# Keeping TensorE on one kind of work between score groups, with 38 late groups in place of 37

## The chip, the cores and the metric

The kernel runs on one core of a Trainium2 chip, in one launch. The metric is the device time of that launch in microseconds. The kernel before takes 457.41 us, the median of 4 runs (457.12 to 457.46).

## The reference

One layer norm feeds two branches, whose results are multiplied. x is 2048 x 448 in bf16, there are 16 heads of 28, and the hidden layer of the second branch has 1792 columns.

```python
xn = layernorm(x)
# branch A: attention
q, k, v = split(xn @ wqkv)                 # 16 heads of 28
p = softmax(q @ k.T * 28 ** -0.5)          # 16 x 2048 x 2048
s = concat_heads(p @ v) @ wo
# branch B: dense, gelu, dense, silu
h = gelu(xn @ w1 + b1)                     # 2048 x 1792
g = silu(h @ w2 + b2)
out = x + s * g
```

## The kernel before

**Tiling.** The queries stand in 4 chunks of 512 columns, the heads in 4 groups of 4 heads (a head takes 32 partitions). One group with one chunk is a block, so there are 16 blocks. A block has 64 score tiles of 128 keys x 512 queries (16 key tiles for each of 4 heads), 1024 in the whole kernel, numbered m. Four tiles in a row, one key tile for the four heads, make a group of four, and there are 256 such groups.

**The exp of a tile** is made in one of two ways. On ScalarE (ACT) one ACTIVATE (L1305, `p_exps`) reads two or three PSUM banks of `ring` and writes as many tiles of P in bf16 (the names P, h and xnT on that line are three places where P slots lie). The ring is split into a set of three banks and a set of two; `p_scores` fills them in turn, and this is called a unit here. The score matmuls (L1249, in `t_score`) of the two or three tiles use different rows of the array and run beside each other. The groups of four that are listed in `QUADS` go the other way, called late groups here: `p_late` brings their four scores into single banks, VectorE (DVE) turns each into a linear form (L1408), and four wide DVE operations of a group (L1468, L1470, L1471, L1472) make three arrays whose sum is the approximate exp; GpSimd (POOL) prepares scaled values of v for them (L1480).

**The other work on TensorE (PE).** `pv_task` and `t_pv` add P times v into the bank `acc` (L1544); a late group takes three products per tile there in place of one. At the end of a block DVE copies `acc` (L1597) and a small chain normalises it (L1604, L1607, L1619, L1626). The first dense layer is L1111, its gelu L1160 on ACT; the second dense layer is L1181, followed by a Tanh on ACT (L1197) for the silu; the q and k projections are L758, v is L1049. The output projection is L1636; DVE multiplies (L1645) and adds x (L1649), and a DMA stores (L1651, L1653). The last block is cut into parts of 256, 128 and 128 queries, whose ends are L1571, L1582, L1585, L1588. L919 is a filler of three matmuls that adds zeros to `acc`; the planner puts it where its own account of PE shows little recent work.

**What sets the order.** The program is planned when it is built. Each piece of work is a generator that offers one `_Task` at a time, with an engine, a duration, a priority (`prio`, smaller is more urgent) and for PE a mode: "row" for scores (four rows of 32), "col" for L1544 and some small sums (four columns of 32), "full" for the rest. `start_of` gives the time at which a task could start by the planner's own account; a change of mode on PE adds `SWITCH` = 0.1 us to it. `run` takes the earliest task, looks at all tasks of that engine that could start within `EPS` = 0.1 us of it, and puts the one with the smallest priority into the engine's program. `pe_mode` is the mode of the last task put on PE. Priorities on PE: unit scores 1, single late scores 0.9, L1544 is 1.2 when it presses (many tiles behind, the end of the kernel, or near the gelu) and 6 otherwise, the first projections 1.5 and 1.6, most of the dense work and L1636 5, L919 95. Every engine runs its own program in order, and semaphores carry the dependencies.

```python
            s0, p0 = min(cand, key=lambda c: (c[0], c[1][3].prio, c[1][0], c[1][1]))
            E = p0[3].E
            near = [c for c in cand if c[1][3].E == E and c[0] <= s0 + EPS]
            s, p = min(near, key=lambda c: (c[1][3].prio, c[1][0], c[0], c[1][1]))
```

Of the kernel before, what the change touches and what calls it, by code (L numbers as in the profile page):

```python
# [11 lines left out]
PE, ACT, DVE, POOL, SP = ET.PE, ET.Activation, ET.DVE, ET.Pool, ET.SP  # L12
# [15 lines left out]
MTOT = NBLK * T * 4  # L28

GM = 64 * 9 + 6  # L30
QUADS = (17, 22, 24, 33, 39, 49, 52, 66, 75, 87, 88, 100, 101, 114, 124, 133, 138, 142, 146, 153, 154, 157, 161, 162, 171, 178, 179, 189, 194, 201, 205, 210, 216, 225, 231, 238, 243)
SM_SCALE = DH ** -0.5
LOG2E = 1.4426950408889634
EXP_C, EXP_LC = 0.1669921875, 1.1155446
# [44 lines left out]
class _Kernel:  # L79
# [132 lines left out]
    def run(self):  # L212
        idle = 0
        while True:
            self.settle()
            if not self.procs:
                return
            cand = []
            for p in self.procs:
                if isinstance(p[3], _Task):  # L220
                    s = self.start_of(p[3])
                    if s is not None:
                        cand.append((s, p))
            if not cand and idle < 100:
                idle += 1
                self.now += 0.1
                continue
            if not cand:
                raise RuntimeError("stuck at %.1f: %s" % (self.now, [(p[0], p[3] if not isinstance(p[3], _Task) else "task") for p in self.procs][:20]))
            s0, p0 = min(cand, key=lambda c: (c[0], c[1][3].prio, c[1][0], c[1][1]))  # L230
            E = p0[3].E
            near = [c for c in cand if c[1][3].E == E and c[0] <= s0 + EPS]
            s, p = min(near, key=lambda c: (c[1][3].prio, c[1][0], c[0], c[1][1]))
            if E == PE and p[3].prio >= 90:
                soon = [c for c in cand if c[1][3].E == PE and c[1][3].prio < 90 and c[0] <= s + p[3].dur]
                if soon:
                    s, p = min(soon, key=lambda c: (c[0], c[1][3].prio))
            idle = 0
            self.now = max(self.now, s)
            self.put(p[3], s)  # L240
            self.advance(p)

    def pe_free(self):
        return self.pe_wait == 0 or not self.late_on

    def ready(self, toks, ahead=0.0):
        return all(b.tw is not None and b.tw <= self.now + ahead for b in toks)

    def build(self):
        nc = self.nc  # L250
        with self.es:
            for E, nm in ((PE, "ev_pe"), (ACT, "ev_act"), (DVE, "ev_dve"), (POOL, "ev_pool"), (SP, "ev_sp")):
                self.evsem[E] = self.sem(nm)
                self.evcnt[E] = 0
            self.alloc()
            self.schedule()
            block = self.es.enter_context(nc.Block())
            for E, attr in ((SP, "sync"), (POOL, "gpsimd"), (DVE, "vector"), (ACT, "scalar"), (PE, "tensor")):
                lst = self.prog[E]

                def run(eng, lst=lst):
                    for f in lst:
                        f(eng)
                getattr(block, attr)(run)
# [129 lines left out]
    def schedule(self):  # L394
# [28 lines left out]
        K.pv_done = [False] * MTOT  # L423
        K.late = {4 * q + k for q in QUADS for k in range(4)}
        K.late_left = [sum(1 for q in QUADS if K.sub_of(4 * q) == b) for b in range(NBLK + 3)]
        K.late_on = False
# [951 lines left out]
    def p_late(self):  # L1378
        K = self
        yield ("until", lambda: K.late_on)  # L1380
        K.spawn(K.p_room(), 0)
        for q in QUADS:
            m0 = 4 * q
# [49 lines left out]
    def assign(self, ms, b0):  # L1433
        K = self
        n = len(ms)
        runs = [list(range(i, i + n)) for i0, w in K.pon for i in range(i0, i0 + w - n + 1)]
        run = min(runs, key=lambda x: (max(K.plast.get(i, -1) for i in x), x[0]))
        for i, m in zip(run, ms):
            K.PB[m] = i
            K.PPREV[m] = K.plast.get(i)  # L1440
            K.plast[i] = m
        K.units.append((ms, b0, run[0]))
# [287 lines left out]
```

## Time and profile before

| | |
|---|---|
| median of 4 runs | 457.41 us |
| the profiled execution: its own time, its span | 457.12 us, 455.3 us |
| ACT busy | 441.2 us (97%), 403 instructions |
| PE busy | 429.1 us (94%), 4389 matmuls |
| DVE busy | 369.6 us (81%), 576 instructions |
| POOL busy | 69.6 us (15%) |
| exps on ACT (L1305) | 195 of two banks, 162 of three |
| filler matmuls on PE (L919) | 357, 30.7 us busy |
| mean granted TensorE clock | 0.996 |

The span is the time from the first instruction to the last in the profiled execution; 1.8 us of the launch lie around it. Busy times of one engine count time in which at least one of its instructions is under way. Instructions of ACT and PE overlap with the next one at their ends, so the mean duration of a row is longer than the distance from one to the next.

### The profile page before, as it was taken

The page shows a single profiled execution, that of the slowest core. Times are in us where ns is not written, and L with a number is a line of the kernel's source. Part 1 is how long each engine was busy: PE and PEld are TensorE (multiplying, and loading weights), DVE is VectorE, ACT ScalarE, POOL GpSimd, SP SyncE. Part 2 cuts the span into 40 slices and gives each one's busy share as a digit, 9 for nine tenths or more (in the row PEclk, how much of TensorE's full clock was granted, in tenths as well). Part 3 has the DMA queues.
Part 4 walks back from the last instruction along what each step waited for, and adds up shares of the span by engine and source line. Part 5 has one row for each costly group of instructions (what it writes and reads, how often), then busy time and mean ns, then how long its engine had stood idle before and what let it go on. Part 6 is the DMA issues. An engine that isn't in the chain of part 4 may idle for free.

```text
span 455.3 us, 10592 instructions
## 1 busy us (share of the span) xinstructions
PE 429.1 (94%) x4389; PEld 160.3 (35%) x4419; DVE 369.6 (81%) x576; ACT 441.2 (97%) x403; POOL 69.6 (15%) x121
## 2 busy tenths in 40 slices
PE   6999999999999999999999999999999999989994
PEld 5543323333233332322334343343332333333552
DVE  8956898958979697968789997078899889888866
ACT  6999999999999999999999999999999999999993
POOL 7470100110020100100000030020011100212210
PEclk9999999999999999999999999999999999999998
DMA  8701000000000000000031000000000000212031
GB/s 277 254 3 37 1 0 1 1 12 2 3 1 0 1 1 3 2 1 1 1 111 35 2 0 1 1 2 0 1 1 2 1 1 8 53 25 42 2 43 42
DMA packets 8049, 11.16 MB, mean 25 GB/s; under 512 B 1697, under 2 KB 6993, under 8 KB 7954
## 3 DMA queue, kind: packets, MB, share of 16 engines
q1 hardware_dynamic: 6850, 8.43, 5.9%
q0 software_dynamic: 864, 1.38, 2.3%
q8 instruction: 35, 0.57, 0.5%
q10 hardware_dynamic: 288, 0.69, 0.4%
q14 instruction: 12, 0.10, 0.1%
HBM read 8.61 MB, written 3.21 MB: 26 GB/s over the span
## 4 chain that ended last, share of the span: by engine, by line
PE 60%; ACT 26%; issue 9%; DVE 3%; DMA 1%; POOL 0%; ACTq 0%; DVEq 0%; POOLq 0%
PE ring L1249 17%; ACT P L1305 14%; PE acc L1544 12%; ACT h L1305 8%; PE ring L1111 7%; PE misc L1181 5%; PE ring L1181 3%; ACT xnT L1305 3%; PE acc L919 2%; PE misc L1111 2%; PE misc L758 2%; PE ring L758 2%; PE ring L1636 2%; PE misc L1636 1%; PE misc L1049 1%
## 5 line engine op out<-in xcount | busy, mean ns | idle before, releaser
L1305 ACT ACTIVATE P<-ring 128x1024 bf16<-128x1024 f32 (+1 forms) x187 | 216.7, 1273 | 1.4 <-PE ring L1249 0.8
L1249 PE MATMUL ring<-qT,kT 32*128 32x512 bf16 (+2 forms) x1084 | 144.9, 358 | 10.7 <-ACT P L1305 3.9
L1305 ACT ACTIVATE h<-ring 128x1024 bf16<-128x1024 f32 (+1 forms) x102 | 118.6, 1269 | 0.4 <-PE ring L1249 0.2
L1249 PEld LDWEIGHTS ring<-qT,kT 32*128 32x128 bf16 x1084 | 37.3, 91 | 133.9 <-ACT P L1305 55.7
L1305 ACT ACTIVATE xnT<-ring 128x1536 bf16<-128x1536 f32 (+1 forms) x68 | 78.7, 1286 | 0.0
L1544 PE MATMUL acc<-P,vaug 128*32 128x512 bf16 (+2 forms) x530 | 49.3, 355 | 0.2 <-DVE E_sb L1597 0.2
L1480 POOL TENSOR_SCALAR cv<-vaug 128x128 bf16<-128x128 bf16 x38 | 26.5, 698 | 134.3 <-PE acc L1544 132.5
L1609 POOL CAST rhi<-rc 128x16 bf16<-128x16 f32 x15 | 7.9, 529 | 202.5 <-DVE rc L1607 168.2
L1111 PE MATMUL ring<-xnT,w 128*128 128x512 bf16 x139 | 35.8, 380 | 2.1 <-issue 1.4
L919 PE MATMUL acc<-ident,zero 128*128 128x128 bf16 x357 | 30.7, 221 | 0.0
L1544 PE MATMUL acc<-h,vaug 128*32 128x512 bf16 x248 | 28.4, 385 | 0.3 <-DVE E_sb L1597 0.3
L1181 PE MATMUL misc<-w,h 128*128 128x448 bf16 x112 | 26.9, 355 | 0.0
L1181 PE MATMUL ring<-w,h 128*128 128x448 bf16 x112 | 26.9, 355 | 0.0
L1249 PE MATMUL misc<-qT,kT 32*128 32x512 bf16 (+1 forms) x68 | 25.3, 377 | 0.0
L919 PEld LDWEIGHTS acc<-ident,zero 128*128 128x128 bf16 x357 | 20.4, 98 | 13.7 <-issue 12.5
L1111 PE MATMUL misc<-xnT,w 128*128 128x512 bf16 x68 | 19.1, 382 | 0.3 <-issue 0.2
L1111 PEld LDWEIGHTS ring<-xnT,w 128*128 128x128 bf16 x152 | 12.2, 97 | 17.7 <-issue 5.6
L1544 PEld LDWEIGHTS acc<-P,vaug 128*32 128x32 bf16 x530 | 12.4, 95 | 15.1 <-issue 12.5
L1544 PE MATMUL acc<-xnT,vaug 128*32 128x512 bf16 (+2 forms) x222 | 17.5, 332 | 0.0
L1408 DVE TENSOR_SCALAR w<-ring 128x512 uint16<-128x512 f32 x17 | 11.7, 686 | 5.8 <-PE ring L1249 5.8
L1160 ACT ACTIVATE h<-h 128x2048 bf16<-128x2048 bf16 (+2 forms) x8 | 16.2, 2020 | 0.0
L1408 DVE TENSOR_SCALAR x_sb<-ring 128x512 uint16<-128x512 f32 x19 | 13.1, 688 | 3.8 <-PE ring L1249 3.6
(284 smaller groups left out, 683.1 us busy)
## 6 DMA issues: line engine op xcount, KB each, us to landing
w<-in_B_w_dram SPq DMA_DIRECT2D x1, 1568.0 KB, 7.2
w<-in_B_w_dram SPq DMA_DIRECT2D x1, 1344.0 KB, 8.2
out_dram<-in_A_x_dram SPq DMA_DIRECT2D x3, 448.0 KB, 10.7
out_dram<-h POOLq DMA_DIRECT2D x6, 224.0 KB, 3.7
x_sb<-in_A_x_dram SPq DMA_DIRECT2D x2, 448.0 KB, 4.6
h<-in_A_wqkv_dram SPq DMA_DIRECT2D x3, 168.0 KB, 4.8
x_sb<-in_A_x_dram ACTq DMA_DIRECT2D x1, 448.0 KB, 4.3
h<-in_A_x_dram SPq DMA_DIRECT2D x1, 448.0 KB, 3.4
```

The costliest lines, as they stand in the source:

```text
L758: ins = eng.matmul(bank, w[:, kt, g * 128:(g + 1) * 128], K.xnT[:, kt, c * 512:(c + 1) * 512], start=(kt == 0), stop=(kt == KT - 1))
L919: ins = eng.matmul(K.acc[:, 0:128], K.zero[:, :], K.ident[:, :], start=False, stop=True, skip_group_check=True)
L1111: ins = eng.matmul(bank, K.w1[:, kt, ft * 128:(ft + 1) * 128], K.xnT[:, kt, c * 512:(c + 1) * 512], start=(kt == 0), stop=(kt == KT - 1))
L1160: yield _Task(ACT, lambda eng, dst=dst, src=src: eng.activation(dst, src, ACTF.Gelu_apprx_tanh), rd, wr, 0.4267 * n + (0.1 if pc else 0.06 ...
L1181: ins = eng.matmul(ps, hv[:, ft, t * 128:(t + 1) * 128], K.w2[:, ft, :], start=(ft == 0), stop=(ft == FT - 1))
L1249: return eng.matmul(dst, K.kT[32 * j:32 * j + 32, g, t * 128:(t + 1) * 128], K.qT[32 * j:32 * j + 32, g, c * 512 + q0:c * 512 + q0 + nq], ...
L1305: return eng.activation(reg[:, i0:i0 + n, :], K.ring[:, b0:b0 + n, :], ACTF.Exp, scale=SM_SCALE)
L1408: yield _Task(DVE, lambda eng: eng.tensor_scalar(K.unit[u][:, 512 * k:512 * k + 512].bitcast(dt.uint16), bank, SM_SCALE * LOG2E * 128.0, ( ...
L1480: yield _Task(POOL, lambda eng, i=i, t=t: eng.tensor_scalar(K.cv[:, i, :], K.vaug[:, t, 4 * g:4 * g + 4, :].rearrange("p h e -> p (h e)"), ...
L1544: return eng.matmul(K.acc[32 * j:32 * j + 32, q0:q0 + nq], w, ap[:, col:col + nq], tile_position=(0, 32 * j), start=(t == 0), stop=(t == T ...
L1609: yield _Task(POOL, lambda eng: eng.tensor_copy(K.rhi[:, :], K.rc[:, :]), [K.b_rc], [K.b_rhl], 1.1, 0.0, 1)
L1636: ins = eng.matmul(ps, K.qT[:, g, c * 512 + t * 128:c * 512 + (t + 1) * 128], K.wo[:, g, :], start=(g == 0), stop=(g == G - 1))
```

## The change

In `run`, the choice among the tasks that could start at about the same time goes by `rate` in place of `prio`. For a PE task with a priority between 1 and 90 (unit scores, single late scores and fillers are not among them), when the last PE task was no score and had another mode than this one, 4 is added. So after L1544 a waiting task of mode "full" counts 4 worse, and after a task of mode "full" a waiting L1544 does, whether it presses or not. After a score all is as before. `QUADS` is a new list with 38 groups in place of 37.

```diff
-QUADS = (17, 22, 24, 33, 39, 49, 52, 66, 75, 87, 88, 100, 101, 114, 124, 133, 138, 142, 146, 153, 154, 157, 161, 162, 171, 178, 179, 189, 194, 201, 205, 210, 216, 225, 231, 238, 243)
+QUADS = (17, 20, 21, 34, 39, 50, 52, 66, 74, 89, 98, 100, 107, 117, 120, 134, 139, 143, 146, 152, 154, 155, 157, 159, 162, 173, 177, 178, 188, 193, 198, 209, 211, 216, 226, 230, 234, 243)
...
-            s, p = min(near, key=lambda c: (c[1][3].prio, c[1][0], c[0], c[1][1]))
+            s, p = min(near, key=lambda c: (self.rate(c[1][3]), c[1][0], c[0], c[1][1]))
...
+    def rate(self, t):
+        p = t.prio
+        if t.E == PE and 1 < p < 90 and self.pe_mode != "row" and t.mode != self.pe_mode:
+            p += 4
+        return p
```

The lines behind the new function stand 6 lines lower in the kernel after (L1249 becomes L1255, L1305 becomes L1311, L1636 becomes L1642).

## The prediction

> **What bounds the kernel now.** I read the page first, then the waits of ACT and of all engines, then the chain and the timeline of single stretches. The page's first lines:
>
> ```profile
> span 455.3 us, 10592 instructions
> PE 429.1 (94%) x4389; PEld 160.3 (35%) x4419; DVE 369.6 (81%) x576; ACT 441.2 (97%) x403; POOL 69.6 (15%) x121
> ```
>
> Both ACT and PE look full. The table of waits, for ACT alone and then for all engines, parts them:
>
> ```profile
> ACT P L1305 <- PE ring L1249: 0.8, 2, 0.5
> ACT P L1305 <- PE misc L1249: 0.2, 1, 0.2
> ACT h L1305 <- PE ring L1249: 0.2, 1, 0.2
> ...
> PEld ring L1249 <- ACT P L1305: 55.7, 137, 0.8
> PEld ring L1249 <- ACT h L1305: 35.3, 84, 0.7
> PEld ring L1249 <- ACT xnT L1305: 20.0, 50, 1.2
> ```
>
> Among the exps ACT waits for scores 1.2 us in all. PE waits 111 us before scores, until an exp has read the banks. So the end is set by a row of 357 exps on ACT; PE sets it only where a score comes late. The pitch of that row comes from the ACT timeline at the end of the kernel (start, length, count of a merged row):
>
> ```profile
> 437.87 8.23 ACT L1305 ACTIVATE P<-ring 128x1536 bf16<-128x1536 f32 x7
> 445.92 2.01 ACT L1305 ACTIVATE xnT<-ring 128x1024 bf16<-128x1024 f32 x2
> 447.73 0.66 ACT L1213 ACTIVATE w<-w 128x448 bf16<-128x448 bf16 x1
> ```
>
> Two exps of two banks take 2.01, and one alone 1.08 (mean of its rows): the second costs about 0.92. The seven before start 8.05 ahead of the next row; four have three banks and three two, so one of three banks costs (8.05 - 3 x 0.91) / 4 = 1.33. Over the whole trace, from end to end, the usual pitch is 0.916 and 1.343. What lies above that pitch, the late scores, is about 3.5 us in all (gelu stretch left out).
>
> How a late score comes about is seen in the chain between 109.7 and 111.8 us, beside ACT's timeline row:
>
> ```profile
> 109.25 4.94 ACT L1305 ACTIVATE h<-ring 128x1536 bf16<-128x1536 f32 x4
> ...
> 109.73 0.32 PE ring L1249 x2
> 110.05 0.97 PE ring L1111 x4
> 111.02 0.43 PE misc L1111 x2
> 111.45 0.32 PE ring L1249 x3
> ```
>
> Between two unit scores PE does six L1111, 1.40 us; with the score 1.72. The four exps (3, 2, 3, 2 banks) would take 1.33 + 0.91 + 1.33 + 1.08 = 4.65 and took 4.94. The same rows price a change of mode: four L1111 after a score take 0.97, two after their like 0.43, so 0.97 - 0.86 = 0.11 for the change.
>
> The tail, from the last exp on, is the end of the chain (there every link counts):
>
> ```profile
> 445.92 1.10 ACT xnT L1305
> ...
> 447.07 1.31 PE ring L1636 x6
> 448.38 0.59 PE acc L1544 x32
> 448.99 0.30 DVE E_sb L1571
> ...
> 449.61 0.97 DVE w L1585
> ...
> 452.23 0.55 DVE h L1645
> 452.77 0.02 issue
> 452.79 0.39 DVE h L1649
> ```
>
> The last exp ends at 447.94, the last DVE operation at 453.2: 5.26 us. The last store ends the span at 455.3.
>
> **The change part by part.** The counts after are read from the instruction order of the two built programs.
>
> *Exps.* 38 groups leave 872 tiles to ACT, not 876: 355 exps in place of 357, two of the two-bank form fewer. 2 x 0.916 = 1.83 us less. Nothing else on ACT changes but the places of the four Tanh (each 5 to 9 exps later). Term: -1.8.
>
> *DVE and POOL.* One group more is four L1408 at 0.69, two operations at 0.69 (L1468, L1472) and two at 1.22 (L1470, L1471), 6.6 us, and one L1480 at 0.70 on POOL. DVE goes to 376 of 454 us. Hidden by DVE's own 86 us of idle time; its buffer is that a late group's sum is taken into `acc` later in its block. If that cover were gone where the groups now stand denser (six between 152 and 162, the second dense layer's stretch), the price is one group, 6.6 us on DVE, some of it seen by PE; the planner's order shows no exp waiting for DVE. Taken as 0.
>
> *L1544.* Eight products more, 4 side by side at 0.216: 0.43 us of PE. Off the path except by late scores.
>
> *Changes of mode.* They fall from 788 to 773. 15 x 0.11 = 1.6 us of PE. The filler L919 stays at 357 matmuls. PE already waits 111 us for ACT, so this is time that becomes waiting: 0 on the path, with -1.6 as its bound if every one stood before a late score. The page "TensorEngine Tiling (Array Packing)" of the Trainium skill says, under Tiling Modes, that a change of tiling mode drains TensorE; this trace shows 0.11 us. Taken alone the rule would credit all 15 and give -1.6 more; the waits above say why I don't.
>
> *Late scores.* I add up, for each pair of successive unit scores, the PE work that is queued between them, by the rows' prices (L1111 and L758 0.216, L1181 and L1636 0.19, four L1544 0.216, L1049 task 0.65 or 0.45, L919 task 0.17, a change of mode 0.11, a score 0.21). Queued on PE behind such work is the unit's score, and ACT waits for that. Leaving out stretches beside a Tanh or the gelu, where ACT gives time, the heavy intervals (1.6 us or more) are:
> before: four of 1.71 to 1.72, which cost 0.07, 0.22, 0.06, 0.15 (mean 0.125); eight of 1.61 to 1.62, which cost 0.65 together (mean 0.08). Sum 1.15.
> after: one of 1.84, five of 1.71 to 1.72, six of 1.62 to 1.65. At 0.125 for 1.71 and that plus the 0.12 more work for 1.84: 0.25 + 0.63 + 0.49 = 1.37.
> So +0.2. Other ways of sorting all intervals (by work alone, or by two, three or four in a row) and pricing each class at its mean before give -0.1 to +0.4. In the gelu stretch PE is full; its work between the scores around it goes from 29.78 to 29.85 us, +0.07. Term for both: +0.2; ends -0.8 (the two heaviest classes cost nothing) and +2.5 (below).
>
> *The tail.* The program ends differently. Before, behind the last unit's score (two banks) stand six L1636, then the last 32 L1544, which start 0.44 after the last exp. After, the last unit has three banks, and between its score and the last L1544 stand 15 L1636: 15 x 0.19 + 0.1 = 2.94 us, with about 0.1 for a wait on the exp in front. The score ends 0.45 after the third-last exp; then come a two-bank and a three-bank exp, 0.90 + 1.33 = 2.23, so the last exp ends 1.78 after the score. The last L1544 start 3.04 - 1.78 = 1.26 after the last exp, 0.8 later than before. Against that, behind the L1544 DVE has one L1645 fewer (-0.55, since that L1636 is done earlier), while two L1645 now end just in front of the copy L1571 (+0.08). Term: +0.3; from 0 (the L1636 find room earlier) to +0.8.
>
> Sum: -1.8 + 0.3 + 0.2 = -1.3 on the profiled execution's 457.12, that is 455.8. That execution is 0.29 under the median, so on the median 457.41 - 1.3 = 456.1.
>
> **The rivals.** A measurement can tell about 0.2%, 0.9 us, from no change: under 456.5 is faster, over 458.3 slower.
> *Longer runs of one kind hold up scores (slower).* With `rate`, work of one kind goes on and the backlog is carried into the next interval. The dearest single late score before cost about 0.3 us (the 4.94 row). If each of the twelve heavy intervals after cost that, 3.6 against 1.15, and the L1181 stretch, where PE has least room, as much again: +2.5 to +3.5, so 458.6 to 459.6. For it: the 1.84 interval stands two units before one of 1.71. Against: most heavy intervals before cost under 0.1, and their number does not rise (twelve and twelve). It decides from +2.5 over my sum, 0.21 for each heavy interval more than taken.
> *The gain is eaten (no change).* Late scores at +1, or the tail at +0.8 and scores at +0.5: 457.0 or so. For it: the tail's 15 L1636 are certain; the net gain is small.
> *PE is the bound after all.* If the 1.6 us of mode changes come off the path and the tail loses nothing: 457.4 - 1.8 - 1.6 + 0.2 = 454.2. For it: PE busy 94%; against: the 111 us of waits, and only the gelu and L1181 stretches are full.
> *The rule does hardly anything.* 15 changes of 788 is 2%; then all comes from the 38th group and the order around it, which is my sum.
>
> **How the numbers follow.** My sum within its smaller errors (454.9 to 456.5) 0.58; PE the bound 0.07; gain eaten (456.5 to 458.3) 0.22; slower 0.13. Faster 0.65, same 0.22, slower 0.13. The range 454.7 to 458.1 leaves out about 0.05 below and 0.14 above.
>
> **What would show it.** Exps: 193 of two banks and 162 of three, the same mean durations; ACT's waits for scores still about 1 us; ACT busy down by some 2. The last exp should end near 446.1 + 0.2 of the span, and the last DVE operation 5.6 after it. L919 at 357 matmuls. I am wrong if ACT waits for scores or for L1544 several us, if exps wait for a P slot, if DVE holds up the late scores, or if the span falls while the last exp does not come earlier.

## The result, and the profile after

The kernel after takes 456.43 us (median of 35 runs, 456.22 to 457.22). The kernel before, run beside it, takes 457.16 us (55 runs, 457.0 to 457.73). The ratio is 0.9985, with a 95% interval of 0.998 to 0.9989: 0.73 us less. That is 0.16%, inside the 0.2% that the prediction took as no change for a single measurement; so many runs make it a small gain that is real. The time lies in the predicted range, 0.3 us above the predicted 456.1. That it comes so near owes 0.25 us to the base: the prediction counted from 457.41, the median of four runs. From 457.16 its -1.3 gives 455.9, so the gain is a little over half of the forecast one; and by the ratio the kernel isn't "faster" as the prediction used the word, though 456.43 lies 0.07 under the 456.5 it named for that. The profiled execution of after took 456.75 us. Its first exp ended 0.42 us later than the first exp of the profiled execution of before. That is scatter: in e3 below, which has the same order of instructions, it ended at 13.79 us, in after at 14.09. It is likely most of why this execution lies 0.3 above its median.

The page of after begins so:

```profile
span 454.9 us, 10630 instructions
PE 429.6 (94%) x4398; PEld 162.1 (36%) x4427; DVE 375.5 (83%) x584; ACT 439.2 (97%) x401; POOL 72.3 (16%) x122
```

Two instructions fewer stand on ACT, and ACT is busy 2.0 us less. DVE has eight more and is busy 5.9 us more. The fillers (now L925) are again 357. The waits of all engines, the rows for exps, gelu and scores (waiting place, releaser, us in all, times, longest):

```profile
PEld ring L1255 <- ACT P L1311: 53.7, 133, 0.8
PEld ring L1255 <- ACT h L1311: 33.4, 78, 0.8
PEld ring L1255 <- ACT xnT L1311: 22.3, 56, 1.1
...
ACT h L1166 <- PE ring L1117: 1.4, 1, 1.4
...
ACT P L1311 <- PE ring L1255: 0.8, 2, 0.5
...
ACT h L1311 <- PE misc L1255: 0.3, 1, 0.3
...
ACT h L1311 <- PE ring L1255: 0.2, 1, 0.2
```

PE still waits 109 us for exps, and the idle time of ACT before exps is 1.3 us against 1.2. Only the gelu's wait stands out, 1.4 us in one place. In before that row is

```profile
ACT h L1160 <- PE ring L1111: 0.8, 2, 0.5
```

These rows show idle time alone and hide the small delays, so I also add up the trace by events. The lateness of an exp is the time from the end of the exp before it to its own end, less the usual pitch of the prediction (0.916 for two banks, 1.343 for three). The gelu stretch runs from the last exp before the first L1166 to the end of the first exp behind the last one. The tail runs from the last exp to the last DVE operation. In us:

| kernel | exps | first exp ends | lateness of all exps | gelu stretch | last exp ends | tail |
|---|---|---|---|---|---|---|
| before | 357 | 13.67 | 3.46 | 30.11 | 447.94 | 5.26 |
| after | 355 | 14.09 | 3.97 | 30.39 | 447.32 | 5.50 |

So after less before: exps -1.83, lateness +0.51, gelu stretch +0.28, tail +0.24. The sum is -0.80, beside -0.73 between the medians. The last links of the chain of waits of after:

```profile
445.18 0.33 PE ring L1255 x12
445.51 0.48 PE ring L1642 x2
...
446.03 0.93 PE ring L1642 x4
446.96 0.76 PE misc L1642 x4
447.71 0.96 PE ring L1642 x5
...
448.70 0.63 DVE h L1651
449.32 0.25 DVE E_sb L1577
```

Behind the last scores stand the 15 output products, and the chain goes through them, where before it had six. The last exp, which ends at 447.32, is no longer in the chain.

### The profile page after: what moved, and what is told of

Its sections match the earlier page's. It is cut to its first block, busy times and chain, and to the rows that moved or that the text cites. A ratio compares the mean times of both kernels' runs of the same rounds, so it can differ in the third digit from the quotient of the medians.

```text
span 454.9 us, 10630 instructions
## 1 busy us (share of the span) xinstructions
PE 429.6 (94%) x4398; PEld 162.1 (36%) x4427; DVE 375.5 (83%) x584; ACT 439.2 (97%) x401; POOL 72.3 (16%) x122
## 4 chain that ended last, share of the span: by engine, by line
PE 50%; ACT 34%; issue 13%; DVE 2%; POOL 1%; ACTq 0%; DVEq 0%; POOLq 0%
ACT P L1311 18%; PE ring L1255 15%; PE acc L1550 10%; ACT h L1311 9%; PE ring L1117 5%; ACT xnT L1311 5%; PE acc L925 2%; PE ring L764 2%; PE misc L1187 2%; PE ring L1187 2%; PE misc L1117 2%; PE ring L1642 1%; PE misc L1642 1%; PE misc L764 1%; PE acc L907 1%
## 5 line engine op out<-in xcount | busy, mean ns | idle before, releaser
L1311 ACT ACTIVATE P<-ring 128x1024 bf16<-128x1024 f32 (+1 forms) x187 | 216.3, 1272 | 1.4 <-PE ring L1255 0.8
L1255 PE MATMUL ring<-qT,kT 32*128 32x512 bf16 (+2 forms) x1087 | 144.6, 358 | 11.7 <-ACT P L1311 5.8
L1311 ACT ACTIVATE h<-ring 128x1024 bf16<-128x1024 f32 (+1 forms) x102 | 117.6, 1253 | 0.7 <-PE misc L1255 0.3
L1255 PEld LDWEIGHTS ring<-qT,kT 32*128 32x128 bf16 x1087 | 37.3, 91 | 134.4 <-ACT P L1311 53.7
L1311 ACT ACTIVATE xnT<-ring 128x1536 bf16<-128x1536 f32 (+1 forms) x66 | 76.9, 1315 | 0.1
L1550 PE MATMUL acc<-P,vaug 128*32 128x512 bf16 (+2 forms) x530 | 47.8, 355 | 0.0
L1117 PE MATMUL ring<-xnT,w 128*128 128x512 bf16 x157 | 40.5, 381 | 1.0 <-issue 0.6
L1187 PE MATMUL misc<-w,h 128*128 128x448 bf16 x140 | 33.2, 355 | 0.1
L1615 POOL CAST rhi<-rc 128x16 bf16<-128x16 f32 x15 | 9.9, 658 | 132.9 <-DVE rc L1613 117.3
L925 PE MATMUL acc<-ident,zero 128*128 128x128 bf16 x357 | 30.5, 221 | 0.0
L1550 PE MATMUL acc<-h,vaug 128*32 128x512 bf16 x248 | 27.4, 384 | 0.0
L925 PEld LDWEIGHTS acc<-ident,zero 128*128 128x128 bf16 x357 | 20.5, 98 | 14.5 <-issue 13.3
L1255 PE MATMUL misc<-qT,kT 32*128 32x512 bf16 (+1 forms) x65 | 24.1, 376 | 0.0
L1414 DVE TENSOR_SCALAR x_sb<-ring 128x512 uint16<-128x512 f32 x27 | 18.6, 688 | 4.6 <-PE ring L1255 4.3
L1414 DVE TENSOR_SCALAR plx<-ring 128x512 uint16<-128x512 f32 x24 | 16.5, 688 | 5.3 <-PE ring L1255 4.9
L1187 PE MATMUL ring<-w,h 128*128 128x448 bf16 x84 | 19.9, 355 | 0.0
L1550 PEld LDWEIGHTS acc<-P,vaug 128*32 128x32 bf16 x530 | 13.0, 95 | 14.6 <-issue 11.8
L1166 ACT ACTIVATE h<-h 128x2048 bf16<-128x2048 bf16 (+2 forms) x8 | 16.2, 2021 | 0.0
L1100 DVE CAST h<-ring 128x512 bf16<-128x512 f32 x19 | 13.1, 688 | 3.7 <-PE ring L1117 3.4
L1550 PE MATMUL acc<-xnT,vaug 128*32 128x512 bf16 (+2 forms) x218 | 16.1, 331 | 0.0
```

Source lines behind the costliest of these rows:

```text
L925: ins = eng.matmul(K.acc[:, 0:128], K.zero[:, :], K.ident[:, :], start=False, stop=True, skip_group_check=True)
L1100: yield _Task(DVE, lambda eng: eng.tensor_copy(dst, bank), [tok], wr, 0.69, 0.0, 2)
L1117: ins = eng.matmul(bank, K.w1[:, kt, ft * 128:(ft + 1) * 128], K.xnT[:, kt, c * 512:(c + 1) * 512], start=(kt == 0), stop=(kt == KT - 1))
L1166: yield _Task(ACT, lambda eng, dst=dst, src=src: eng.activation(dst, src, ACTF.Gelu_apprx_tanh), rd, wr, 0.4267 * n + (0.1 if pc else 0.06 ...
L1187: ins = eng.matmul(ps, hv[:, ft, t * 128:(t + 1) * 128], K.w2[:, ft, :], start=(ft == 0), stop=(ft == FT - 1))
L1255: return eng.matmul(dst, K.kT[32 * j:32 * j + 32, g, t * 128:(t + 1) * 128], K.qT[32 * j:32 * j + 32, g, c * 512 + q0:c * 512 + q0 + nq], ...
```

## The experiments

Each kernel below is the kernel after with one edit, where nothing else is said. All times are medians; ratios are to the kernel before, run on the same chip.

### The rule alone and the list alone

e1 keeps the list of before and adds `rate`; e2 keeps the new list and chooses by `prio`.

```diff
 e1:  QUADS = (17, 22, 24, 33, 39, 49, ...)      # the 37 groups of before
 e2:  s, p = min(near, key=lambda c: (c[1][3].prio, c[1][0], c[0], c[1][1]))
```

e1, expected: 

> The old list of 37 groups with the new choice rule. Two exps of the before kernel now stand, by the instruction order, behind a product that PE reaches only after 7 and after 16 more tasks (exp 278 behind five L1181 tasks, exp 299 behind twelve fillers); the PE work queued between the scores around the gelu grows from 30.1 to 32.8 us. Theory (rule and list fit each other; ACT's row of exps is the bound, and it is held where PE puts a product late): the two exps late by 2 to 3 us each and the gelu stretch by 1 to 2.7: +5 to +8, 462 to 465 us. Rival (fewer changes of mode are worth PE time on the path, the list does little): 773 changes as in the after kernel, so about the after kernel's time without the 38th group, 456 to 458 us.

e2, expected: 

> The new list of 38 groups with the old choice rule. 355 exps; changes of mode 811; exp 235 stands behind nine PE tasks past its own score, seven of them L1181 tasks (2.7 us) and a product; the PE work around the gelu is 33.5 us in place of 30.1. Theory: -1.8 for the two exps, +2 to +3 for that exp, +2 to +3.4 for the gelu stretch, so 459.5 to 462 us. Rival (the 38th group alone brings the gain): 456 to 456.5 us.

e1 took 466.88 us, ratio 1.021 [1.0196, 1.0224], and e2 464.62, ratio 1.0167 [1.0153, 1.0181]. Each half alone loses, 9.7 and 7.5 us, and together they win 0.7. Both went the way that was expected and further. In the account, e1 has a lateness of 10.75 in place of 3.46 and a gelu stretch of 32.64; e2 a lateness of 7.43 and a gelu stretch of 33.79, and its last store ended the span 3.3 us behind the last DVE operation. The waits of ACT in e1 show what kind of lateness it is:

```profile
ACT P L1311 <- PE acc L1550: 4.0, 2, 3.7
ACT xnT L1311 <- PE acc L1550: 3.2, 1, 3.2
```

These exps did not wait for a score. They waited for a product L1550 that had not yet read the P slot into which they write; no exp of after or of before waits for that. The PE rows ahead of the two waits (start, length, count):

```profile
361.08 1.69 PE L1187 MATMUL ring<-w,h 128*128 128x448 bf16 x8
...
389.39 2.18 PE L925 MATMUL acc<-ident,zero 128*128 128x128 bf16 x36
```

In the first place PE does eight dense products in a row while a product that presses is put off; in the second it does 36 fillers, since the planner had no other work for PE that could start there. These two exps end 3.3 and 3.9 us later than the pitch has it, 7.2 of the 7.3 us by which e1's lateness is over that of before. e2 has one such exp, 3.1 late, behind eight L1181 (310.14 to 311.8).

What follows: a list of late groups belongs to one rule of choice. The effect of the rule can't be read from the change as a whole, nor from the count of mode changes: e1 has 773, as few as after, and is the slowest kernel of all.

### Two tiles on one row of the array

A head has a fixed row of the array. Where a late tile is computed in the same go as a unit's score, it may need a row that the unit uses as well. In the kernel after this is so for 26 units, in before for 22, by the programs as they are built (the expectations count 25 and 23). e3 (from after) and e5 (from before) compute such a late tile on a free row, with the q and k of the head that lives there; the order of instructions stays, and the values of these tiles are another head's.

```diff
+        row, free = {}, [j for j in range(4) if all(p[2] != j for p in ps)]
+        for i, p in enumerate(ps):
+            if free and p[0] in K.late and any(o[2] == p[2] for o in ps[:i]):
+                row[p[0]] = free.pop(0)
...
+                j = row.get(m, j)
```

e3, expected: 

> The after kernel, every instruction in the same place, but in the 25 unit scores in which two tiles use the same rows of the array the late group's tile is computed on a free row (with another head's data, so its values are another head's). Such a unit score should take 0.32 in place of 0.53 us. Theory (the late scores that I missed are backlog from units joined by a colliding late tile): the lateness of all scores above the usual pitch falls from 4.0 to about 3.2 us, the time by 0.6 to 1.0, to 455.4 to 455.8 us. Rival (backlog comes from the dense work between scores, collisions are hidden): lateness within 0.1 of 4.0, the time within 0.2 of the after kernel, 456.3 to 456.6.

e5, expected: 

> The before kernel, every instruction in its place, with the same edit as e3: in the unit scores in which a late group's tile shares its rows with another tile (23, two of them with five tiles, which cannot all be freed) that tile is computed on a free row, with another head's data. Theory (what the after kernel lost in late scores is collisions; the rest is alike in both): the lateness falls from 3.5 to 2.0 to 2.2 us, the time by 1.2 to 1.5, to 455.6 to 456.0, and the distance to e3 (454.5) grows to 1.2 to 1.4, the gain that I forecast. Rival (the before kernel hid its collisions; the after kernel is later for another cause): lateness 3.0 or more, the time 456.7 to 457.2.

e3 took 454.51, ratio 0.9942 [0.9929, 0.9954]: 1.92 less than after, twice what was expected, so the theory names the cause and has it too small. Its lateness is 1.96 in place of 3.97. e5 took 455.61, ratio 0.9977 [0.9964, 0.9989]: 1.55 less than before, as expected, with a lateness of 1.85 in place of 3.46. Three of its eight executions took 457.05 to 457.25, for a reason that isn't known; the median and the trace are of the other five. The distance to e3 is 1.10, a little less than the 1.2 to 1.4 expected. The timeline shows the mechanism at one unit. In the kernel after:

```profile
109.44 0.39 PE L1255 MATMUL ring<-qT,kT 32*128 32x512 bf16 x3
109.67 0.37 PE L1255 MATMUL misc<-qT,kT 32*128 32x512 bf16 x1
...
110.08 3.71 ACT L1311 ACTIVATE h<-ring 128x1536 bf16<-128x1536 f32 x3 [0.28 <-PE misc L1255]
```

and the same four tiles in e3:

```profile
108.83 0.39 PE L1260 MATMUL ring<-qT,kT 32*128 32x512 bf16 x3
108.84 0.39 PE L1260 MATMUL misc<-qT,kT 32*128 32x512 bf16 x1
```

On four rows the fourth matmul starts 0.01 us behind the three, on a shared row 0.23 us behind them. The unit then takes about 0.53 us in place of 0.32, and the exp behind it waited 0.28.

What follows: the shared rows cost after 2.0 us of lateness and before 1.6. Of the +0.51 by which the lateness grew, 0.40 is theirs; without them the two kernels differ by 0.11.

### The gelu stretch

In e4 the single late scores of the gelu stretch take 128 of their 512 columns, so the late tiles of that stretch hold sums that are in part not computed.

```diff
+        short = len(ms) == 1 and prio == 0.9 and K.in_gelu()
...
+                nq = 128 if short else nq
```

Expected: 

> The after kernel, in the same order, but the single late scores within the gelu stretch compute 128 of their 512 columns (the rest of the bank keeps old values). It takes about 0.15 us from each of some 19 PE tasks, up to 2.9 us. Theory (in the gelu stretch PE is the bound, so work there goes straight to the end): ACT's waits among the gelus, 1.5 us in the after kernel, fall to 0.1 to 0.3, and the time by 1.1 to 1.4, to 455.0 to 455.3 us. Rival (the one long wait, 1.4 us, comes from the order of the banks or from DVE): at most -0.3, 456.1 to 456.5 us.

It took 455.39, ratio 0.9962 [0.995, 0.9975]: 1.04 less than after. The gelu stretch went from 30.39 to 29.37 and ACT's wait in it from 1.4 to 0.3; the lateness elsewhere stayed (4.00). That is a little less than expected. It is also for less PE work than the 2.9 us of 19 scores: two pairs of them run beside each other, and behind three more the next matmul starts no earlier. 14 times some 0.155 us is about 2.2 us of PE work, which bought 1.04 us: the stretch waits for PE first and then for ACT's own work.

### What a change of mode is worth

e7 changes no mode. It adds about as much PE work as a change costs, at 31 of the 35 places where work of mode "full" directly follows work of mode "col" (28 times L1550): two matmuls of 128 columns with weights of zero, 62 in all.

```diff
+        if t.E == PE and t.mode == "full" and self.pe_mode == "col" and t.ps is not None:
+            def more(eng, ps=t.ps):
+                for _ in range(2):
+                    eng.matmul(ps[:, 0:128], self.zero[:, :], self.ident[:, :], start=False, stop=False, skip_group_check=True)
+            self.prog[PE].append(more)
...
```

`t.ps` is the bank that the task writes; it is entered where such tasks are made.

Expected: 

> The after kernel with the same order, and two matmuls of 128 columns with zero weights (0.11 us together, about the price of a change of mode) in front of each of 31 tasks at which PE changes from column mode to full mode (17 dense ones, 14 fillers): 3.4 us more on PE, as if those changes cost twice. Theory (ACT's row is the bound; a change of mode counts only just before a late score): +0.1 to +0.8 us, 456.5 to 457.2. Rival (PE is the bound, a change of mode counts in full, and the fewer changes are what the rule brings): +2.5 to +3.4, 458.9 to 459.8.

It took 457.88, ratio 1.0022 [1.0011, 1.0032]: 1.45 more than after, between what the two theories expected, and neither holds. The times scatter (457.52 to 460.15); by the spans, median 455.8 against 454.55, it is 1.25. At one of the places the trace has (L159 is the added work, L933 a filler)

```profile
163.15 0.28 PE L159 MATMUL acc<-ident,zero 128*128 128x128 bf16 x2
163.28 0.33 PE L933 MATMUL acc<-ident,zero 128*128 128x128 bf16 x3
```

From start to start this is 0.12 us at each place, a little over the 0.11 that was meant. 31 places are 3.8 us of PE work, so a microsecond of it cost 0.38 us of time (0.33 by the spans). The lateness took 1.24 of it (5.21 in place of 3.97); the gelu stretch took none. e3 gives nearly the same price: 26 units at 0.21 us are 5.5 us of PE work, for 1.92 us of time, 0.35. What a change of mode itself does to the time no run measures apart from the order; that it counts like this added work is argued.

### The end of the kernel without the rule

In e6 the rule ends when all scores are done, so that only the order of the last pieces changes.

```diff
-        if t.E == PE and 1 < p < 90 and self.pe_mode != "row" and t.mode != self.pe_mode:
+        if t.E == PE and 1 < p < 90 and self.next_m < MTOT and self.pe_mode != "row" and t.mode != self.pe_mode:
```

Expected: 

> The after kernel, with the penalty for a change of kind switched off once the last unit score is queued; only the tail changes: the last 32 L1544 stand behind 9 matmuls of L1636 in place of 15, and one L1645 more comes behind them on DVE. Theory (the tail's chain counts link by link): the last L1544 start 1.1 us earlier, but the reciprocal (L1585) waits for two more L1636 on PE and one more L1645 on DVE, so the end comes 0.1 to 0.3 earlier: 456.1 to 456.4 us. Rival (the queue of L1636 in front of the last product sets the tail alone): -0.8 to -1.1, 455.3 to 455.7.

It took 457.94, ratio 1.0016 [1.0008, 1.0025]: 1.5 more than after, where less was expected. The tail itself did what was forecast: the last DVE operation came 5.31 us after the last exp in place of 5.50. But the span ended 3.8 us after that operation, in place of 2.1. The stores show why. The timeline of POOL and of SP's queue, of after:

```profile
449.62 0.87 POOL L1659 DMA_DIRECT2D out_dram<-h  x1 [6.72 <-DVE E_sb L1577]
451.88 1.29 SPq L1657 DMA_DIRECT2D out_dram<-h  x2
```

and of e6:

```profile
451.60 0.87 POOL L1659 DMA_DIRECT2D out_dram<-h  x1 [8.75 <-DVE h L1655]
451.63 1.29 SPq L1657 DMA_DIRECT2D out_dram<-h  x2
```

POOL's last store, 224 KB that are added to what lies in memory, starts 2.0 us later, since the DVE product that feeds it now stands behind most of the normalisation (450.69 to 451.3, in after 448.7 to 449.3; in both the store starts 0.3 us behind it, though the rows name other DVE work that ended later). Such a store needs some 4 us from issue to landing (median 4.0; SP's of 112 KB 1.8 in after). It landed at 455.6, and the last of SP's, which ran beside it and took 3.3 us where it took 1.65 in after, at 455.9. In after they landed at 453.3 and 454.5. My expectation ended with DVE and left out the slower of the two queues.

### Lists that fit, with and without the rule

Four kernels put what e3 showed into the plan: a unit's score with a shared row is entered with 0.43 us. For each a list of late groups is sought anew, e8 with the rule, e9 to e11 without it (e10 and e11 from a second, as long search). e8, e9 and e10 have 37 groups, e11 has 36.

```diff
 all four:
+        most = max(sum(p[2] == j for p in ps) for j in range(4))
-        return _Task(PE, fall, rd, tok_of, 0.218 + 0.001 * len(fl), ...
+        return _Task(PE, fall, rd, tok_of, (0.218 if most < 2 else 0.43) + 0.001 * len(fl), ...
 e8:
+QUADS = (17, 21, 23, 34, 38, 49, 56, 67, 70, 92, 98, 100, 108, 117, 123, 135, 140, 143, 146, 148, 149, 155, 159, 162, 173, 176, 182, 190, 192, 197, 209, 213, 218, 226, 230, 234, 244)
 e9, e10, e11, which choose by prio in place of rate:
+QUADS = (16, 18, 28, 35, 38, 50, 57, 66, 71, 90, ...)
+QUADS = (16, 19, 28, 36, 39, 50, 57, 66, 72, 88, ...)
+QUADS = (17, 21, 25, 36, 45, 49, 58, 65, 67, 72, ...)
```

e8, expected: 

> The kernel after, but a unit's score in which two tiles share a row of the array is entered in the plan with 0.43 us in place of 0.218, so that the plan avoids such pairs, and another list of 37 late groups goes with it (357 exps on ACT, as in the kernel before). By the two programs: 21 unit scores with a shared row against 25 in the kernel after, 710 changes of mode on PE against 773, seven heavy intervals of PE work (1.6 us or more) between two unit scores against twelve, PE work in the gelu stretch 26.5 us against 30.15, 309 fillers against 357. Theory (late scores, shared rows and changes of mode on PE are paid at about 0.4 us of time for 1 us of PE work, and the gelu stretch goes down to what ACT needs): two exps more +1.8; late scores 3.97 to about 2.2, -1.8; gelu stretch 30.4 to about 29.1, -1.3; tail -0.1 to -0.2. Sum -1.5 against the kernel after: 454.9, with 454.0 to 455.6. The rival of the forecast (changes of mode and PE work are hidden, only the count of exps acts) expects +1.8: 458.2.

e9, expected: 

> The kernel of e8_fitted_new with the choice by priority alone, as in the kernel before (no account of the last kind of work), and a list of 37 late groups sought for that choice for about as long. By its program: 357 exps, 21 unit scores with a shared row, 716 changes of mode, seven heavy intervals, two of them of 2.1 and 2.4 us, PE work in the gelu stretch 27.8 us, 285 fillers. If the choice by kind brings nothing of its own and all comes from a list that fits, it takes what e8_fitted_new takes, within 0.4. If keeping to one kind brings time also with a fitted list (theory), it takes 0.5 to 1.5 more than e8_fitted_new: about 455.4 to 456.4.

In these two texts the changes of mode, the heavy intervals and the PE work of the gelu stretch are counted too low, because the products of L1544, which stand one line lower there, were left out. Rightly counted, e8 has 773 changes (as many as after), eleven heavy intervals and 28.7 us of work in the gelu stretch, and e9 has 803, nine and 30.7. So e8's expectation went by a gelu stretch with 26.5 us of PE work, which the program doesn't have.

e10, expected: 

> As e9_fitted_old (choice by priority alone, shared rows entered in the plan), with a list of 37 groups from a longer search. By its program: 357 exps, 17 unit scores with a shared row (e9: 21, e8: 21), 812 changes of mode, eight heavy intervals, PE work in the gelu stretch 30.3 us (e9 30.7, e8 28.7). If the rule has no worth of its own and e9's list was only a bad find, this one comes to within 0.4 of e8_fitted_new's 454.97. By the account (lateness 1.7 against 2.6, gelu stretch 30.5 to 31.1 against 28.9, the same tail) it takes 0.7 to 1.3 more than e8: 455.7 to 456.3.

e11, expected: 

> As e9_fitted_old, with a list of 36 groups from a search that began at e8's list. By its program: 359 exps (195 of two banks, 163 of three, one of one bank), 29 unit scores with a shared row, one of it with seven tiles, 794 changes of mode, thirteen heavy intervals, PE work in the gelu stretch 28.5 us, as little as e8's 28.7. It asks whether the short gelu stretch needs the rule: if so, the stretch stays over 30 us; by the PE work it takes 28.7 to 29.2. In all, against e8: exps +1.8, lateness about +0.3, gelu 0, tail -0.3 to 0: 456.5 to 457.1.

e8 took 454.97, ratio 0.9951 [0.9938, 0.9965]: 1.46 less than after and 2.2 less than before. Of the kernels that leave nothing out it is the fastest. e9 took 456.72, ratio 0.9989 [0.998, 0.9998]; e10 455.72, ratio 0.9967 [0.9956, 0.9979]; e11 456.62, ratio 0.9986 [0.9977, 0.9995]. The accounts:

| kernel | exps | lateness | gelu stretch | PE work in it | tail |
|---|---|---|---|---|---|
| before | 357 | 3.46 | 30.11 | 30.1 | 5.26 |
| after | 355 | 3.97 | 30.39 | 30.2 | 5.50 |
| e1 (rule alone) | 357 | 10.75 | 32.64 | 32.8 | 4.79 |
| e2 (list alone) | 355 | 7.43 | 33.79 | 33.5 | 5.65 |
| e8 (with the rule) | 357 | 2.60 | 28.93 | 28.7 | 4.99 |
| e9 (without) | 357 | 1.86 | 31.51 | 30.7 | 4.99 |
| e10 (without) | 357 | 1.88 | 30.45 | 30.3 | 4.99 |
| e11 (without) | 359 | 3.10 | 28.93 | 28.5 | 4.50 |

The PE work is that of the instructions between the scores around the stretch, at the prices of the prediction. In e11 the one exp of a single bank is entered at 0.49, the two-bank pitch less the 0.43 between three banks and two.

e8 against after: two exps more +1.83, lateness -1.37, gelu stretch -1.46, tail -0.51. That is -1.51, where the expectation had -1.5 from terms of +1.8, -1.8, -1.3 and about -0.15. The sum fits in part by luck: the lateness fell 0.4 us less than expected, the tail 0.36 more. e9 against e8: lateness -0.74, gelu stretch +2.58, together +1.84 beside 1.75 measured, more than either expectation had. e10 against e8: -0.72 and +1.52, together +0.80 beside 0.75, as expected. In both the difference is the gelu stretch, where ACT waits for PE. In e9:

```profile
ACT h L1166 <- PE ring L1117: 1.2, 2, 0.8
ACT h L1166 <- PE ring L1611: 1.0, 1, 1.0
```

In e8 and e11 no gelu waits, and both stretches take 28.93 us: that is ACT's own work there. In all eight kernels the gelu stretch is as long as the PE work in it, within 0.5 us but for e9.

What follows: e11 has the short gelu stretch without the rule, so the rule isn't what makes it short. It is the list: e8 and e11 put 17 and 13 single late scores there, e9 and e10 20 and 21. Their number isn't all of it: before has only 16 and 30.1 us of work, with nine tasks of L1544 where e8 and e11 have six. Changes of mode count there too: e8 has 27 in the stretch, e10 33, e2 47. Without the rule e9 and e10 have the smaller lateness, with 30 and 39 changes of mode more than e8. The best kernel has the rule, and the best without it is 0.75 us behind (on another chip; the intervals of the two ratios overlap), but one list for the one side and three for the other can't tell a worth of the rule from the luck of a search. What is shown is that e8, with the price for shared rows and a list sought anew, brings more than the change did. Which of the two does it is open: no run has a list sought as e8's was without that price, and e8 still has 20 units with a shared row, where after has 26.

## Why the prediction was right or wrong

**Exps (-1.8): right.** 193 of two banks and 162 of three stand in the trace of after, and the account gives -1.83.

**DVE and POOL (0): right.** DVE is busy 5.9 us more, and no exp waits for DVE.

**The tail (+0.3): right.** It grew by 0.24, from 5.26 to 5.50, and by the path that was named: the 15 output products between the last score and the last L1550.

**Late scores and gelu (+0.2): wrong in size.** They came to +0.51 and +0.28, 0.6 more than the term for both. The step that failed is the price "a score 0.21", the same for every unit. A unit with a shared row takes 0.53 in place of 0.32, and after has 20 of these with four tiles where before has 12. e3 and e5 put 0.40 of the 0.51 on that. The heaviest interval after, which I priced at 0.25, stands ahead of the score at 109.44 that was shown; its exp was 0.39 late, and in e3, with the same work ahead of it, 0.19. For the gelu the step was to go by the sum of the PE work (+0.07, and rightly counted +0.05). The sum was right, but the stretch grew by 0.28: one gelu waited 1.4 us at once, where before two waited 0.8 together. Why the wait gathered in one place no run tests. Lateness and gelu put the last exp 0.6 us behind the 446.3 that was named; it ended at 447.32, and the other 0.42 is the later first exp. The sign that it named, ACT's waits for scores at about 1 us, held (1.3) and told nothing of this.

**Changes of mode (0): wrong in the argument.** I held that PE's waits of 111 us would take up whatever is saved. e7 shows that time on PE is neither hidden nor all on the path: it counts by a little over a third. If changes of mode count like it, 15 are worth 15 x 0.11 x 0.38 = 0.6 us, an estimate. That is no further term of the sum, since what changes of mode do to the scores is in the lateness already. The Trainium skill (page "TensorEngine Tiling (Array Packing)", section Tiling Modes) says that a change of mode drains TensorE; credited in full at this trace's 0.11 us each, that would have been 1.6.

**Small slips.** The four Tanh stand 2 to 9 exps later, not 5 to 9. The lower end of the term for late scores, -0.8, is about -0.6 by the prediction's own figures (0.49 in place of 1.15, and +0.07). Neither carries the result. The median of before was taken as 0.29 above its profiled execution; over 55 runs it is 0.04.

**The rivals.** "The gain is eaten" came nearest: it named scores at +0.5, and the tail held to +0.24 in place of its +0.8. Its sum was about -0.4, the forecast's -1.3, and -0.73 was measured. "Longer runs of one kind hold up scores" doesn't show in after, and with the other list it shows with a price that I hadn't thought of: in e1 the rule holds up products, exps wait for P slots 3.2 and 3.7 us at a time, and the kernel takes 9.7 us more. "The rule does hardly anything" is refuted by e1 and e2; my reason, that 15 changes of 788 are 2%, counted the wrong thing, since a plan made in order takes another course after the first other choice. "PE is the bound after all" is not what happened: PE is busy 0.5 us more and the time fell, and 3.8 us more of PE work in e7 cost 1.45.

## What to carry to other kernels

Where two engines are both nearly full, work taken from the one with waits is worth a share of its length; measure that share by adding a known amount of work to the plan as it stands, as e7 did, before you set it to nothing or to the whole. A list that was sought under one rule of choice is no base for judging another rule: seek both again, and look at what the instruction order does in the tightest stretch. At the end of a kernel, follow each store to its landing, on each queue, and not only the last arithmetic.

## What was not expected of the hardware

- Matmuls of 32 rows in one go run beside each other only on different rows of the array: the fourth starts 0.01 us behind the others on a free row and 0.23 us behind them on a shared one.
- A change of mode costs about 0.11 us of PE (from the prediction's rows); as time of this kernel, if it counts like the work added in e7, about 0.04 us.
- The store that adds to memory from POOL's queue takes about 4 us for 224 KB from issue to landing; when it was issued 2.0 us later (e6), the 112 KB store of SP beside it took 3.3 us in place of 1.65, and the span ended 1.5 us later.
